# Block-sparse attention and a two-layer MoE in one kernel: four heads' denominators in one matmul group, row maxima moved by DMA, a shorter weight conversion and a new order of work

## The chip, the cores and the metric

One core of one Trainium2 chip runs the whole kernel. The metric is device time in microseconds (us); lower is better. Matrix multiplies run on TensorE (PE), whose weight loads the profile lists on their own (PEld); element-wise work runs on VectorE (DVE), ScalarE (ACT) and GpSimd (POOL); SyncE (SP) issues all DMAs from one queue, in order.

## The reference, cut to what matters

```python
B, H, S, D = 4, 8, 768, 64            # batch, heads, sequence, head dimension; blocks of 32
scores = q @ k.T / sqrt(D)
mask = band | first and last block row and column | 3 sampled blocks per block row
scores = where(mask, scores, -1e9); scores -= max(scores, axis=-1)
attn = exp(scores); attn /= sum(attn, axis=-1) + 1e-9
x = (attn @ v) put together to (B*S, 512)
h = x @ w_in                           # 512 -> 2048
out = (h * clip(h + 3, 0, 6) / 6) @ w_out   # 2048 -> 512
```

q, k and v come as 32-bit floats; w_in and w_out come as 64-bit floats and are turned into a high and a low 32-bit part on the chip.

## The kernel before, in words

The kernel makes products of 32-bit numbers from pairs of parts (hi and lo) in TensorE's fp32r form, and uses plain fp32 matmuls, which the trace shows as two records each, where the weights of the softmax are summed.

**Attention** is cut into 64 units u0 to u63: one head of one half of the queries of one batch, the head counting fastest. Eight units share a batch and a half. A unit loads q, k and v (loadq, loadk, loadv), splits them (qh, kh, qb on ACT, ql on DVE, kl on POOL into KB), and then:

- m_0 to m_2: scores of 128 queries each against all 768 keys, for the block maxima; the weights of these matmuls are QA, the moving side is KA (L611 to 620).
- r_0 to r_2, fin_0, fin_1: DVE reduces them to maxima of 24 blocks, adds the block mask and reduces to the negated maximum of each query, a 128x3 tile MN (mneg).
- mt and qm: three matmuls of MN against the identity turn the maxima into a row in PSUM, and ACT copies it into row 96 of QB (L638 to 644). There are two MN tiles and two QB tiles for each half.
- s_0 to s_2, e_0 to e_2: scores with the keys on the partitions, two matmuls per block of 128 keys: KA with QA, and KB with QB. The second brings in the low parts, the mask (rows 64 to 87) and the negated maximum (row 96). ACT takes the exponential.
- av: the product with v. In the first WIDE = 16 units the weights are 128 columns wide, v beside ones, so that the denominators come out of the same matmuls. From u16 on v alone, 64 columns, is laid on the two halves of the array in turn, and DVE sums the exponentials over the key blocks (suma, sumb, sumc).
- From u16 on, dm sums those over the partitions with a 128x64 matrix of ones, two heads (a pair) to the two column halves, dc copies to SBUF, and rc takes the reciprocal of 128x384 on DVE. Pairs in the list COMPACT gather one row per head to 128x6 by DMA first (rg), take the reciprocal of that, write it to DRAM (rs) and read it back spread over 64 partitions (rb).
- ux_0 to ux_2 multiply and split the result x for the MoE.

**The MoE** is cut into 64 steps m0 to m63: eight steps of two chunks of 128 hidden columns for each batch and half. h_ is x by w_in (hi by hi, lo by hi, hi by lo), ga, gb, gh and gl are the gate and its split on ACT, DVE, ACT and POOL, and o_ is the product with w_out into three output banks. The high parts of the weights stay in SBUF. The low parts are written to DRAM and loaded again for each step (loadin, loadout, four buffers each), except that chunks in the list DIRECT stay where they are for the first use.

**The weights** are 32 chunks w0 to w31 (L478 to 523): load the 64-bit words, size (ACT, absolute value of the high word), clamp (DVE), bits_0 to bits_2 (DVE, integer operations that put the bits of the 32-bit number together), high (ACT), low (the subtraction that leaves the low part; on POOL, or on DVE for chunks in the list QUICK), save (DMA).

**The order** is a text, SCORE, that names unit or step and operation one after the other; every engine and the DMA queue get their instructions in the order of this text, and nothing reorders them after. PSUM holds two big tiles of two banks for scores, MoE hidden columns, maxima and denominators, one bank for av and three for the output. An engine's instruction that waits holds up all behind it, and this holds for SyncE's DMAs as well.

All operations are recorded by one helper, so that the profile puts them all on line L359; they are told apart by the tiles that they write and read.

Of the kernel before, what the change touches and what calls it, by code (L numbers as in the profile page):

```python
# [908 lines left out]
```

## Time and profile before

| | us |
|---|---|
| three runs | 1034.07, 1035.63, 1036.9 (median 1035.63) |
| the profiled execution | 1036.67 |
| its span, first to last instruction | 1034.9 |
| PE busy in it | 985.5 (95%) |
| DVE, ACT, POOL busy | 711.8 (69%), 503.8 (49%), 279.8 (27%) |
| DMA moved | 148.27 MB, mean 143 GB/s |

A row of instruction groups reads: line, engine, operation, tiles written <- read, shape, count, then total busy us, mean ns of one, and the engine's idle time before them with what ended it. A row in order of time has the start in us, the duration and the same names. Matmuls overlap each other, so the spacing of their starts, not their duration, tells what one costs.

### The profile page before, as it was taken

What the parts mean: (1) busy time and instruction counts of PE and PEld (TensorE: products, weight loads), DVE (VectorE), ACT (ScalarE), POOL (GpSimd) and SP (SyncE); (2) the same over time, 40 slices, a digit from 0 to 9 for tenths busy, and PEclk for the clock granted to TensorE, in tenths of its full rate; (3) what the DMA queues carried; (4) which work ended last, traced back from release to release, by engine and by line L of the source; (5) the groups of instructions that cost most, each with busy time, mean ns of one, the idle gap of its engine ahead of it and who ended that gap; (6) DMA issues with size and microseconds to landing.
All of it is one profiled execution on the core that took longest, in us unless ns stands there. A gap on an engine that the chain in (4) does not pass through costs nothing.

```text
span 1034.9 us, 13289 instructions
## 1 busy us (share of the span) xinstructions
PE 985.5 (95%) x4904; PEld 783.4 (76%) x4904; DVE 711.8 (69%) x929; ACT 503.8 (49%) x781; POOL 279.8 (27%) x172
## 2 busy tenths in 40 slices
PE   4888999999999999999999999999999999999998
PEld 3565677778777777877888777778788877778986
DVE  5888789797667687677665768675867767864111
ACT  5677666555545454545443553453554455443121
POOL 4232334333223132222221322222222222221222
PEclk9998899999999999999999999999999999999999
DMA  5666657685534444433553444434434444413432
GB/s 159 189 185 198 186 188 211 208 259 159 168 100 120 145 142 133 135 102 120 142 166 99 136 128 145 127 111 120 153 112 132 133 136 152 123 58 106 143 112 91
DMA packets 119668, 148.27 MB, mean 143 GB/s; under 512 B 59667, under 2 KB 68755, under 8 KB 119604
## 3 DMA queue, kind: packets, MB, share of 16 engines
q1 hardware_dynamic: 119604, 147.44, 47.4%
q8 instruction: 38, 0.62, 0.3%
q14 instruction: 26, 0.21, 0.1%
HBM read 132.69 MB, written 14.70 MB: 142 GB/s over the span
## 4 chain that ended last, share of the span: by engine, by line
PE 70%; DVE 15%; DMA 5%; issue 4%; ACT 4%; SPq 0%; POOL 0%; POOLq 0%; DVEq 0%; ACTq 0%
PE big L359 41%; PE out L359 20%; PE av L359 10%; DVE xhl L359 5%; DVE acc L359 4%; DVE bm L359 2%; DVE rec L359 1%; ACT pr L359 1%; DMA kraw<-kT 1%; DMA wraw<-w_out 1%; DMA win_lo<-xhl 1%; DMA qraw<-qT 1%; DVE g L359 1%; DVE QA L359 1%; DMA wraw<-w_in 1%
## 5 line engine op out<-in xcount | busy, mean ns | idle before, releaser
L359 PE MATMUL big<-xhl,win_hi 128*128 128x384 f32 x1024 | 268.2, 343 | 1.9 <-DVE bm L359 1.9
L359 POOL TENSOR_TENSOR glo<-g,ghi 128x768 fp32r<-128x768 f32 x64 | 119.2, 1863 | 413.8 <-ACT ghi L359 401.3
L359 POOL TENSOR_TENSOR kb<-kraw,KA 64x768 fp32r<-64x768 f32 x64 | 124.8, 1950 | 273.2 <-ACT KA L359 238.2
L359 PEld LDWEIGHTS big<-xhl,win_hi 128*128 128x128 f32 x1024 | 183.0, 188 | 18.6 <-issue 7.8
L359 DVE TENSOR_REDUCE bm<-big 128x24 f32<-128x768 f32 x168 | 158.6, 953 | 55.8 <-PE big L359 53.7
L359 ACT ACTIVATE pr<-big 128x768 f32<-128x768 f32 x192 | 152.0, 811 | 87.8 <-PE big L359 86.5
L359 PE MATMUL av<-pr,vo 128*64 128x384 f32 (+1 forms) x768 | 176.7, 496 | 0.4 <-ACT pr L359 0.4
L359 PE MATMUL big<-xhl,wlo_in 128*128 128x384 f32 x512 | 172.3, 336 | 0.0
L359 PE MATMUL out<-wout_hi,ghi 128*128 128x512 f32 x384 | 154.1, 401 | 0.0
L359 PE MATMUL out<-wout_hi,glo 128*128 128x512 f32 x384 | 151.9, 396 | 0.2 <-POOL glo L359 0.2
L359 PE MATMUL out<-wlo_out,ghi 128*128 128x512 f32 x384 | 151.8, 395 | 0.0
L359 PE MATMUL big<-QA,KA 128*128 128x384 f32 x384 | 140.4, 366 | 4.6 <-ACT pr L359 3.8
L359 PE MATMUL big<-qb,kb 97*128 97x384 f32 x384 | 136.0, 354 | 4.6 <-ACT qb L359 4.6
L359 DVE SCALAR_TENSOR_TENSOR g<-g,big 128x768 f32<-128x768 f32 x64 | 60.8, 951 | 101.7 <-ACT g L359 101.4
L359 PEld LDWEIGHTS av<-pr,vo 128*64 128x64 f32 (+1 forms) x768 | 75.7, 152 | 64.4 <-issue 45.5
L359 PE MATMUL big<-KA,QA 128*128 128x384 f32 x336 | 92.9, 364 | 21.9 <-ACT xhl L359 11.4
L359 ACT ACTIVATE g<-big,half_b 128x768 f32<-128x768 f32 x64 | 57.7, 902 | 104.6 <-PE big L359 96.4
L359 PEld LDWEIGHTS big<-KA,QA 128*128 128x128 f32 x336 | 59.4, 192 | 53.5 <-issue 13.3
L359 PEld LDWEIGHTS big<-xhl,wlo_in 128*128 128x128 f32 x512 | 96.2, 188 | 0.0
L359 PEld LDWEIGHTS big<-QA,KA 128*128 128x128 f32 x384 | 75.8, 198 | 20.6 <-ACT pr L359 9.6
L359 DVE TENSOR_TENSOR acc<-pr 128x768 f32<-128x768 f32 x48 | 52.4, 1091 | 55.9 <-ACT pr L359 55.3
L359 PEld LDWEIGHTS out<-wout_hi,glo 128*128 128x128 f32 x384 | 72.1, 188 | 17.6 <-POOL glo L359 0.6
(67 smaller groups left out, 1136.1 us busy)
## 6 DMA issues: line engine op xcount, KB each, us to landing
wlo_out<-wout_lo SPq DMA_DIRECT2D x125, 256.0 KB, 2.7
wlo_in<-win_lo SPq DMA_DIRECT2D x120, 256.0 KB, 2.7
kraw<-kT SPq DMA_DIRECT2D x64, 384.0 KB, 3.5
qraw<-qT SPq DMA_DIRECT2D x64, 192.0 KB, 2.8
vo<-vP SPq DMA_DIRECT2D x64, 192.0 KB, 3.0
wraw<-w_out SPq DMA_DIRECT2D x16, 512.0 KB, 4.3
wraw<-w_in SPq DMA_DIRECT2D x16, 512.0 KB, 4.0
out_dram<-wraw SPq DMA_DIRECT2D x24, 256.0 KB, 2.9
```

The source lines that it names most:

```text
L359: return lambda *a, **k: tc.keep_in_program_order(op(*a, **k))
```

## The change

- The first 12 units, not 16, have the wide av.
- Denominators: the four heads of a quad (units 4i to 4i+3) are summed by four matmuls with 32 columns of ones, each onto the 32 partitions that belong to its head, after the sums of all four. Beyond the first 12 units the reciprocal always goes the compact way: four DMAs gather one row per head to 128x12, DVE takes the reciprocal of that, one DMA writes it to DRAM, and each pair reads its two rows back with two broadcasting DMAs. All six pairs of the wide units are in COMPACT. The buffers acc and uu grow to 5 and 4.
- Row maxima: a matmul m_t takes the queries t, t+3, t+6 and so on, so that partition p of MN holds queries 3p to 3p+2. From unit 10 on (BYDMA) one DMA writes the 128x3 maxima into row 96 of QB; the three matmuls and ACT's copy remain for units 0 to 9.
- Weights: size multiplies the high word by 2 to the power -112 instead of taking its absolute value; clamp is gone; bits_0 only shifts, and bits_2 takes the sign alone. All 32 subtractions (low) run on DVE, and only chunks 0 to 3 are used directly.
- SCORE is new from beginning to end.

```diff
-WIDE = 16
-QUICK = "4 6 8 14 17 18 22 30"
-DIRECT = "0 2 3 4 10 11 12 16 18 23 28"
-COMPACT = "1 3 5 7 13 21"
+WIDE = 12
+BYDMA = 10
+QUICK = "0 1 2 3 4 5 6 7 8 9 10 11 12 13 14 15 16 17 18 19 20 21 22 23 24 25 26 27 28 29 30 31"
+DIRECT = "0 1 2 3"
+COMPACT = "1 3 5 7 9 11"
 SCORE = """
...
-    ones = const.tile([P, D], F32, name="ones")
-    MN = [const.tile([P, NT, 2], F32R, name=f"mneg{i}") for i in range(2)]
+    ones = const.tile([P, 32], F32, name="ones")
+    MN = [const.tile([P, 2, NT], F32R, name=f"mneg{i}") for i in range(2)]
...
         def size(self):
...
-            act.activation(out=self.wf, in_=self.raw[:, :, 1].bitcast(F32), func=AF.Abs)
-
-        def clamp(self):
-            dve.tensor_scalar(out=self.wf, in0=self.wf, scalar1=2.0 ** -15, scalar2=None, op0=ALU.max)
+            act.mul(out=self.wf, in_=self.raw[:, :, 1].bitcast(F32), mul=2.0 ** -112)
...
-                dve.tensor_scalar(out=wi, in0=wi, scalar1=0x07FFFFFF, scalar2=3, op0=ALU.bitwise_and, op1=ALU.logical_shift_left)
+                dve.tensor_scalar(out=wi, in0=wi, scalar1=3, scalar2=None, op0=ALU.logical_shift_left)
...
             if op == "dm":
-                out.append((prev, "sumc"))
+                out += [(at(units, self.n - i), "sumc") for i in (3, 2, 1)]
+            if op == "rb" and not self.wide:
+                before = ""
+                out.append((self.last, "rs"))
+            if op == "mt" and self.n >= BYDMA:
+                before += " qb"
...
-                pe.matmul(out_j, lhsT=self.QA[:, t * P:(t + 1) * P], rhs=self.KA[:, j * HALF:(j + 1) * HALF], start=True, stop=True)
+                pe.matmul(out_j, lhsT=self.QA[:, t:HALF:NT], rhs=self.KA[:, j * HALF:(j + 1) * HALF], start=True, stop=True)
...
         def mt(self):
+            if self.n >= BYDMA:
+                dma.dma_start(out=self.QB[96:97].bitcast(F32).rearrange("o (p t) -> o p t", t=NT), in_=MN[self.n % 2].bitcast(F32)[:, 0])
+                return
             self.mtp = big_tile()
...
         def qm(self):
-            act.copy(out=self.QB[96:97], in_=self.mtp[0:1, 0, :HALF])
+            if self.n < BYDMA:
+                act.copy(out=self.QB[96:97].rearrange("o (p t) -> o t p", t=NT), in_=self.mtp[0:1, 0, :HALF].rearrange("o (t p) -> o t p", t=NT))
...
         def dm(self):
+
             self.den = big_tile()[:, 0, :HALF]
-            for side, acc in enumerate(pair_accs.pop(self.pair)):
-                pe.matmul(self.den[64 * side:64 * side + 64], lhsT=ones, rhs=acc, start=True, stop=True)
+            for i, acc in sorted(quad_accs.pop(self.quad).items()):
+                pe.matmul(self.den[32 * i:32 * i + 32], lhsT=ones, rhs=acc, start=True, stop=True)
...
         def rg(self):
 
-            if self.n in compact:
-                self.spread = sb.tile([P, HALF // 64], F32, name="spread")
-                for i in (0, 64):
-                    dma.dma_start(out=self.spread[i:i + 64], in_=self.rec[i:i + 1].rearrange("o (a c) -> o a c", a=64))
+            heads = 2 if self.wide else 4
+            if self.n in compact or not self.wide:
+                self.spread = sb.tile([P, heads * HALF // P], F32, name="spread")
+                for i in range(heads):
+                    p0 = P // heads * i
+                    dma.dma_start(out=self.spread[p0:p0 + P // heads], in_=self.rec[p0:p0 + 1].rearrange("o (a c) -> o a c", a=P // heads))
...
         def rb(self):
...
+            row, each, first = self.row if self.wide else self.last.row, 64 if self.wide else 32, 0 if self.wide else self.n % 4 - 1
+            if not self.wide:
+                self.rec = sb.tile([P, HALF], F32, name="rec")
+            for i in range(2):
+                one = row[each * (first + i):each * (first + i + 1)].rearrange("a c -> (a c)").rearrange("(o n) -> o n", o=1)
+                dma.dma_start(out=self.rec[64 * i:64 * i + 64], in_=one.to_broadcast([64, HALF]))
```

In the built program the order below is read engine by engine. Each row is one instruction, or several equal ones in a row; the names are the tiles' names, with a buffer number where two rows would read alike, and L359 of the kernel before is L356 after.

More of the change, by code (lines that the diff above doesn't have):

```diff
@@ L464, in mq @@
             for t in range(NC):
-                pe.matmul(self.mqp[:, 0, t * NB:(t + 1) * NB], lhsT=self.ind_r[:, t * P:(t + 1) * P], rhs=self.mval[:, 64:88], start=True, stop=True)
+                pe.matmul(self.mqp[:, 0, t * NB:(t + 1) * NB], lhsT=self.ind_r[:, t // NT * HALF + t % NT:(t // NT + 1) * HALF:NT], rhs=self.mval[:, 64:88], start=True, stop=True)
         def rows(self):
@@ L478, in fused_kernel @@
     class Weight(Work):
-        NEEDS = {"size": "load", "clamp": "size", "bits_0": "clamp", "bits_1": "bits_0", "bits_2": "bits_1", "high": "bits_2", "low": "high", "save": "low"}
+        NEEDS = {"size": "load", "bits_0": "size", "bits_1": "bits_0", "bits_2": "bits_1", "high": "bits_2", "low": "high", "save": "low"}
         def __init__(self, src, hi, lo_d):
@@ L507, in bits @@
             else:
-                dve.scalar_tensor_tensor(out=wi, in0=high, scalar=-0x40000000, in1=wi, op0=ALU.bitwise_and, op1=ALU.bitwise_or)
+                dve.scalar_tensor_tensor(out=wi, in0=high, scalar=-0x80000000, in1=wi, op0=ALU.bitwise_and, op1=ALU.bitwise_or)
         def high(self):
@@ L548, in __init__ @@
             self.early = 0 < n <= H
+            self.quad = (b, h // 4, hf)
         def needs(self, op):
@@ L666, in sumc @@
         def sumc(self):
-            self.acc = sb.tile([P, HALF], F32, name="acc", bufs=3)
-            pair_accs.setdefault(self.pair, []).append(self.acc)
+            self.acc = sb.tile([P, HALF], F32, name="acc", bufs=5)
+            quad_accs.setdefault(self.quad, {})[self.n % 4] = self.acc
             dve.tensor_tensor(out=self.acc, in0=self.acc2[:, 0], in1=self.acc2[:, 1], op=ALU.add)
@@ L686, in uc @@
             if self.side == 0:
-                pair_u[self.pair] = sb.tile([P, HALF], F32, name="uu")
+                pair_u[self.pair] = sb.tile([P, HALF], F32, name="uu", bufs=4)
             act.copy(out=pair_u[self.pair][self.mine], in_=self.avt[self.mine])
@@ L846, in fused_kernel @@
     units = [Unit(n, *u) for n, u in enumerate(units)]
+    for x in units:
+        x.last = units[x.n // 4 * 4 + 3]
     steps = [Step(n, n // NFP // 2, n // NFP % 2, n % NFP) for n in range(NU)]
```

589 lines of the change are left out of this document (292 added, 297 removed).

## The prediction

> **What bounds the kernel now.** I read the page's first lines, then the busy time by stage, then the groups of instructions, and last the order of time inside the long middle stage. The page says which engine is full:
>
> ```profile
> PE 985.5 (95%) x4904; PEld 783.4 (76%) x4904; DVE 711.8 (69%) x929; ACT 503.8 (49%) x781; POOL 279.8 (27%) x172
> ```
>
> TensorE matmuls (PE) are in flight 95% of the span, but that is an average. The busy time by stage (columns: stretch, its length, then PE, weight loads, VectorE, ScalarE, GpSimd with their counts, granted clock, DMA share, GB/s) splits it:
>
> ```profile
> 0.00:260.00 260.00, 224.31 (x958) 172.41 (x959) 208.87 (x321) 158.03 (x255) 90.09 (x72) 0.96 0.64 195
> 260.00:936.00 676.00, 666.15 (x3479) 527.94 (x3478) 482.64 (x585) 323.59 (x499) 169.44 (x89) 1.00 0.43 128
> 936.00:1035.00 99.00, 94.98 (x471) 83.01 (x469) 20.30 (x23) 22.21 (x28) 20.27 (x11) 1.00 0.36 112
> ```
>
> In the first 260 us, where the weights are converted, PE idles 35.7 us, VectorE (DVE) is busy 80% and the clock is 0.96; none is full, and steps wait for each other. From 260 to 936 us PE idles 9.9 us of 676: this stage is bound by the number and length of matmuls. From 936 on there is only MoE work, which the change leaves alone. So the rule for the sum is: a matmul removed after 260 us is worth its full spacing, DVE and ScalarE time removed there is worth little, and in the first stage a saving counts only in part.
>
> The profiled execution took 1036.67 us, 1.8 more than its span of 1034.9; the median of the three runs is 1035.63. I sum against 1036.67.
>
> **The change part by part.** First the path of the row maxima, one unit of it in order of time (start, duration, engine):
>
> ```profile
> 506.15 0.96 DVE L359 TENSOR_REDUCE bm<-big 128x24 f32<-128x768 f32 x1 [0.54 <-PE big L359]
> 506.18 0.39 PE L359 MATMUL out<-wlo_out,ghi 128*128 128x512 f32 x1
> 506.41 0.39 PE L359 MATMUL out<-wout_hi,glo 128*128 128x512 f32 x1
> 507.14 0.23 DVE L359 TENSOR_TENSOR bm<-bm,mq 128x72 f32<-128x72 f32 x1
> 507.41 0.23 DVE L359 TENSOR_REDUCE mneg<-bm 128x3 fp32r<-128x72 f32 x1
> 509.46 0.34 PE L359 MATMUL big<-ident,mneg 128*2 128x128 f32 x3
> 509.64 0.57 PE L359 MATMUL big<-xhl,win_hi 128*128 128x384 f32 x2
> 509.84 0.47 ACT L359 CAST qb<-big 1x384 fp32r<-1x384 f32 x1 [0.48 <-PE big L359]
> 510.75 0.34 PE L359 MATMUL big<-QA,KA 128*128 128x384 f32 x1
> 510.93 0.34 PE L359 MATMUL big<-qb,kb 97*128 97x384 f32 x1
> ```
>
> The maxima are ready 0.23 us after 507.41. Three small matmuls move them to a row (start 509.46), the next ordinary matmul starts at 509.64, so they take 0.18 us of PE, and ScalarE's copy ends at 510.31. The scores start afterwards; their matmuls are 0.18 us apart (510.75, 510.93), and the wider ones of the MoE output 0.23 (506.18, 506.41). The change does this for units 10 to 63 by a DMA. Removed: 54 x 0.18 = 9.7 us of PE. Where these matmuls and their copies go, PE, before (unit 24 and, behind it, unit 23; QB of unit 24 is qb_108):
>
> ```order
> L359 MATMUL big<-ident,mneg_117 2x128 x3
> L359 MATMUL big<-xhl,win_hi 128x384 x2
> L359 MATMUL big<-xhl,wlo_in 128x384
> L359 MATMUL big<-xhl,win_hi 128x384 x2
> L359 MATMUL big<-xhl,wlo_in 128x384
> L359 MATMUL big<-ident,mneg_118 2x128 x3
> L359 MATMUL big<-xhl,win_hi 128x384 x2
> L359 MATMUL big<-xhl,wlo_in 128x384
> L359 MATMUL big<-xhl,win_hi 128x384 x2
> L359 MATMUL big<-xhl,wlo_in 128x384
> L359 MATMUL big<-QA,KA 128x384
> L359 MATMUL big<-qb_108,kb_110 128x384
> ```
>
> And after, the end of the stretch that leads to unit 24's scores:
>
> ```order
> L356 MATMUL big<-qb_107,kb_111 128x384
> L356 MATMUL out_2394<-wout_hi,ghi 128x512
> L356 MATMUL out_2394<-wlo_out,ghi 128x512
> L356 MATMUL out_2394<-wout_hi,glo 128x512
> L356 MATMUL out_2395<-wout_hi,ghi 128x512
> L356 MATMUL out_2395<-wlo_out,ghi 128x512
> L356 MATMUL out_2395<-wout_hi,glo 128x512
> L356 MATMUL av<-pr,vo_120 64x384 x6
> L356 MATMUL big<-acc,ones 32x384 x4
> L356 MATMUL big<-QA,KA 128x384
> L356 MATMUL big<-qb_108,kb_110 128x384
> ```
>
> The identity matmuls have gone, and the denominators come as four heads of 32 columns. Between unit 24's last score block for the maxima and its first row of qb_108 now stand 12 score matmuls (12 x 0.18 = 2.2 us), 9 of the output (9 x 0.23 = 2.1), one set of AV and one denominator.
>
> ```profile
> L359 PE MATMUL big<-acc,ones 128*64 128x384 f32 x96 | 26.1, 501 | 1.3 <-DVE acc L359 1.1
> L359 PE MATMUL av<-pr,vo 128*64 128x384 f32 x576 | 104.7, 494 | 0.0
> L359 PE MATMUL av<-pr,vo 128*128 128x384 f32 x192 | 71.9, 504 | 0.4 <-ACT pr L359 0.4
> L359 PE MATMUL big<-ident,mneg 128*2 128x128 f32 x192 | 22.2, 225 | 8.4 <-DVE mneg L359 8.4
> L359 PEld LDWEIGHTS big<-acc,ones 128*64 128x64 f32 x96 | 7.2, 135 | 13.5 <-issue 6.0 <-DVE acc L359 5.9 <-ACT qb L359 0.4
> L359 DVE RECIPROCAL rec<-rec 128x384 f32<-128x384 f32 x26 | 66.3, 2550 | 14.4 <-ACT rec L359 14.1
> ```
>
> PE stood 8.4 us before the identity matmuls until the maxima were ready; of this, between 260 and 936 us (waits: total, times, longest):
>
> ```profile
> PE big L359 <- DVE mneg L359: 1.4, 3, 0.7
> ```
>
> I count only these 1.4 us.
>
> Denominators: 96 records for 24 pairs take 26.1 us, 1.09 a pair in flight. In order of time one pair takes less:
>
> ```profile
> 834.05 0.81 PE L359 MATMUL big<-acc,ones 128*64 128x384 f32 x4
> 834.80 0.44 PE L359 MATMUL big<-QA,KA 128*128 128x384 f32 x1
> 835.55 2.55 DVE L359 RECIPROCAL rec<-rec 128x384 f32<-128x384 f32 x1 [0.22 <-ACT rec L359]
> ```
>
> Four records start at 834.05 and the next matmul at 834.80: 0.75 us for two heads, though one record alone lasts 0.50; so the two column tiles ran beside each other. If four tiles of 32 columns do the same, a group of four heads costs what a pair did. 24 pairs at 0.75 to 1.09 become 13 groups (units 12 to 63) at the same: 11 x 0.75 to 11 x 1.09, 8.3 to 12.0 us; I take 10, nearer the group's mean since some pairs are torn apart by a wait. Weight loads of ones waited 5.9 us for the sums (DVE acc); with 13 places instead of 24, and the quad's first three sums long done, I take 3 of it as saved.
>
> The Trainium skill, page "TensorEngine Tiling (Array Packing)", section "Key Properties", says that a change of tiling mode drains the array. A 32-column group behind a 64-column AV would pay this where today's pair runs on. No row shows that switch; at the 0.18 us that a whole group of narrow identity matmuls takes, 13 of them would give 2.3 us back.
>
> AV: units 12 to 15 leave the 128-column form. 71.9 us / 16 = 4.49 a unit, against 104.7 / 48 = 2.18: 4 x 2.31 = 9.2 us. They lie in the first stage, where PE has idle time, so the worth is between 0 and 9.2; I take 4.
>
> The reciprocals of 128x384 (66.3 us of DVE) shrink to small ones, as do ScalarE's copies of the maxima and half the denominator copies. After 260 us PE hides all of it: worth 0. What is late in its place is the trip through DRAM:
>
> ```profile
> spread<-rec SPq DMA_DIRECT2D x12, 1.5 KB, 3.2
> rec<-spread SPq DMA_DIRECT2D x6, 3.0 KB, 2.6
> ```
>
> Two hops of some 3 us and a broadcast, which the pairs in COMPACT make already. The first MoE step that reads the result comes several units later; worth 0.
>
> Weight conversion, first stage, in rows of DVE and GpSimd:
>
> ```profile
> L359 DVE TENSOR_SCALAR xhl<-xhl 128x512 f32<-128x512 f32 x32 | 17.0, 531 | 7.8 <-ACT xhl L359 7.4
> L359 POOL TENSOR_TENSOR xhl<-xhl,wout_hi 128x512 f32<-128x512 f32 x12 | 15.3, 1288 | 24.5 <-issue 12.2 <-ACT wout_hi L359 11.7 <-POOL kb L359 0.6
> L359 DVE TENSOR_TENSOR xhl<-xhl,win_hi 128x512 f32<-128x512 f32 x5 | 6.0, 1201 | 0.0
> L359 DVE TENSOR_TENSOR wlo_in<-xhl,win_hi 128x512 fp32r<-128x512 f32 x2 | 1.4, 692 | 0.6 <-ACT win_hi L359 0.5
> L359 DVE TENSOR_TENSOR acc<-acc,pr 128x768 f32<-128x768 f32 x48 | 59.4, 1238 | 15.1 <-ACT pr L359 13.2
> L359 DVE TENSOR_TENSOR acc<-pr 128x768 f32<-128x768 f32 x48 | 52.4, 1091 | 55.9 <-ACT pr L359 55.3
> L359 DVE TENSOR_TENSOR acc<-acc 128x384 f32<-128x384 f32 x48 | 45.1, 940 | 1.4
> L359 DVE TENSOR_TENSOR uu<-av,tmp 64x384 f32<-64x384 f32 x48 | 26.5, 553 | 8.1 <-ACT tmp L359 6.9
> ```
>
> Removed on DVE: 32 clamps, 17.0 us, and three reciprocals of 2.55 (pairs ending with units 9, 11, 15), 7.7. Added: 24 subtracts that GpSimd did (1.29 each), at 0.69 to 1.20: 16.6 to 28.8; and the sums and merges of units 12 to 15, 4 x (1.09 + 1.24 + 0.94 + 0.55) = 15.3. Net +7 to +19 us on DVE over 260, against 24 x 1.29 = 31 us less on GpSimd. The first chunk before, on DVE:
>
> ```order
> L359 TENSOR_TENSOR bm<-bm,mq 128x72
> L359 TENSOR_REDUCE mneg_117<-bm 128x3
> L359 TENSOR_SCALAR xhl<-xhl 128x512 x3
> L359 SCALAR_TENSOR_TENSOR xhl<-wraw,xhl 128x512 x2
> L359 TENSOR_SCALAR xhl<-xhl 128x512
> L359 SCALAR_TENSOR_TENSOR xhl<-wraw,xhl 128x512 x2
> ```
>
> And after:
>
> ```order
> L356 TENSOR_TENSOR bm<-bm,mq 128x72
> L356 TENSOR_REDUCE mneg_117<-bm 128x3
> L356 SCALAR_TENSOR_TENSOR xhl<-wraw,xhl 128x512
> L356 TENSOR_SCALAR xhl<-xhl 128x512
> L356 SCALAR_TENSOR_TENSOR xhl<-wraw,xhl 128x512
> L356 TENSOR_TENSOR wlo_in<-xhl,win_hi 128x512
> L356 SCALAR_TENSOR_TENSOR QA<-qraw,QA 64x384
> ```
>
> The clamp has left the chain of TENSOR_SCALARs and the subtract into wlo_in has joined behind the last bit operation: the chain of one weight chunk no longer goes round by GpSimd. A chunk's chain gets shorter (0.53 and 0.6 less), DVE's queue a little longer. I take 0 for the first stage, between -15 (if half of PE's 35.7 us of idle time goes with the shorter chain) and +12 (if two thirds of the added DVE time shows).
>
> The new cost is the DMA for the maxima. It stands in SyncE's one queue, here for unit 24:
>
> ```order
> L356 DMA wlo_in<-win_lo_89 128x512
> L356 DMA vo_119<-vP 128x6x64
> L356 DMA wlo_out<-wout_lo_102 128x512
> L356 DMA qb_108<-mneg_117 1x128x3
> L356 DMA qraw<-qT 128x384
> L356 DMA vo_120<-vP 128x6x64
> L356 DMA spread<-rec 32x1x12 x4
> L356 DMA kraw<-kT 128x768
> ```
>
> The transfer of qb_108 stands behind a load of low weights, which waits until PE has read the old ones, and ahead of the next q, v and k loads, which it holds up until the maxima are ready; those are wanted a unit later. How long the queue stands at such loads today:
>
> ```profile
> SPq L359 <- PE big L359: 239.9, 131, 7.5
> SPq L359 <- PE out L359: 236.7, 108, 10.6
> ```
>
> That is 239.9/131 = 1.8 and 236.7/108 = 2.2 us each. The need from the last block of scores to the landed row: 0.96 + 0.23 + 0.23 and a landing like the small spread's, 3.2: 4.6 us. Cover for unit 24: 2.2 + 2.1 + 2.2 (AV) + 0.75 = 7.2 us. Counting rows in the same way, most units have 6 to 10 us and the least two (19 and 63) some 4.9. So it is mostly hidden, and shows at the narrow ones if a load of 2 us holds the queue. I take 3 us in all, from 0 to 54 x 0.5 = 27.
>
> Last, the weight side of the maxima's own matmuls now steps over three columns (QA at stride 3). No row here shows a strided weight load. Below nothing is excluded (no work is removed). Bound by the rows that exist:
>
> ```profile
> L359 PEld LDWEIGHTS big<-KA,QA 128*128 128x128 f32 x336 | 59.4, 192 | 53.5 <-issue 13.3 <-ACT xhl L359 11.4 <-DVE bm L359 10.0
> L359 PEld LDWEIGHTS av<-pr,vo 128*64 128x64 f32 x576 | 38.6, 136 | 47.7 <-issue 43.7 <-ACT QA L359 1.0 <-DVE acc L359 0.7
> L359 PEld LDWEIGHTS big<-ident,mneg 128*2 128x2 f32 x192 | 13.1, 83 | 22.9 <-DVE mneg L359 8.6 <-issue 6.9 <-PE av L359 1.2
> ```
>
> 83 ns for 2 columns, 136 for 64, 192 for 128: about 0.85 ns a column, so reading at half speed would add 0.11 us to each of 6 x 64 = 384 loads, 42 us if all of it shows, 14 if a third of it does, 0 if the load still ends under the matmul before. I take 0. The Trainium skill, page "SBUF — State Buffer", in the note on cachelines in the section "Door 1: The DMA port swizzle", speaks against the change: lines are 16 bytes and at least two hits on a line are wanted, and 12-byte steps give four accesses in three lines; the same note calls strides up to 4 fp32 free. By the first half the sum would rise by the strided rival's price below, by the second by nothing.
>
> Sum: 1036.7 - 9.7 - 1.4 - 10 - 3 - 4 + 0 + 3 = 1011.6, so 1011.
>
> **The rivals.** (a) The first stage gains as well: shorter chunk chain, GpSimd off the shared work, -15: 996. For it: PE idle there 35.7 us; against: DVE gets 7 to 19 us more to do. (b) The first stage loses: +12, 1023. (c) The strided loads show by a third: +14, 1025; wholly, +42, 1053. (d) The four 32-column tiles do not run beside each other, so that the change does not do what it says: two tiles at a time cost 13 more pairs, 13 x 0.75 = 10 us, one at a time about 20: 1021 to 1031. (e) The other side: the maxima land late. Each unit whose landing exceeds its cover stops PE at the first row of qb; 54 units at 0.52 us eat all 28.1 us, at 1 us they make 1036.7 - 28.1 + 54 = 1063. With a cover of 7.2 it decides at a landing of 7.2 - 1.4 + 0.5 = 6.3 us after the maxima instead of 3.2, that is if the queue usually stands 3 us more with them ready. Against it: the loads ahead mostly wait for PE work that stands before the scores anyway.
>
> **How the numbers follow.** Forecast 1011, chance 0.58; (a) 0.13; (b) 0.08; (c) 0.07 by a third and 0.02 wholly; (d) 0.03; (e) 0.09. A difference under 0.3% (3.1 us) is about what a measurement of this kernel cannot tell from none. Faster by more: the forecast, (a), (b), the milder (c) and (d): 0.89. Within: (e) where it just eats the gain, 0.05. Slower: the rest of (e) and (c) wholly, 0.06. The range reaches from (a), 996, past (b) and the milder (c) into (d), 1028; the unknown costs (AV 0 to 9, denominators 8 to 12, maxima 0 to 27) lie in it but for the end of the last.
>
> **What would show it.** Right: no identity matmuls after unit 9; denominators in 13 groups with eight records in about 0.75 us; PE idle after 260 us still about 10 us and that stage about 20 us shorter; 384-column matmuls for the maxima still 0.18 apart; landing of the mneg row about 3 us. Wrong: PE waits for the DMA of qb that sum to over 10 us, weight loads of QA above 0.2 us with matmuls spread to match, or a first stage whose 260 us move by more than 12.

## The result, and the profile after

Four runs of the changed kernel took 998.31 to 1003.93 us, median 999.4, beside 1034.07 to 1036.9, median 1035.47, of the kernel before: ratio 0.966, 95% interval 0.9627 to 0.9692. That is 11.6 us below the forecast of 1011, near rival (a), a first stage that gains as well. The profiled execution took 998.31 us, span 996.5, against 1036.67 and 1034.9. The engines, from the page:

```profile
PE 954.3 (96%) x4750; PEld 772.0 (77%) x4750; DVE 649.4 (65%) x924; ACT 468.2 (47%) x712; POOL 248.8 (25%) x148
```

To compare stages they have to end at the same work. I cut both traces at the first matmul of MoE step m9 and of step m57. The first cut is not quite the same work: ahead of it the changed kernel has the 12 score matmuls of unit 17, some 2.2 us at 0.18 each, which the kernel before has behind it. The busy time by stage, before:

```profile
0.00:256.80 256.80, 221.11 (x939) 169.31 (x940) 207.16 (x319) 157.56 (x254) 88.69 (x72) 0.96 0.64 195
256.80:954.60 697.80, 687.95 (x3595) 546.67 (x3594) 492.03 (x596) 330.64 (x509) 174.53 (x92) 1.00 0.43 127
954.60:1035.00 80.40, 76.39 (x373) 67.39 (x372) 12.64 (x15) 15.64 (x18) 16.58 (x9) 1.00 0.38 118
```

And after:

```profile
0.00:244.20 244.20, 214.33 (x935) 166.09 (x936) 194.06 (x326) 153.53 (x245) 58.03 (x48) 0.96 0.71 216
244.20:917.00 672.80, 664.15 (x3446) 538.61 (x3446) 442.70 (x584) 299.04 (x449) 174.17 (x91) 1.00 0.48 138
917.00:997.00 80.00, 75.80 (x373) 67.28 (x371) 12.65 (x15) 15.64 (x18) 16.57 (x9) 1.00 0.40 119
```

The first stage is 12.6 us shorter, the middle 25.0, and the rest, up to the spans' ends, 0.8 (80.3 against 79.5). With unit 17's scores on the same side of the cut it would be some 15 and 23. In the middle PE's idle time is 9.9 us before and 8.7 after: the gain there is hardly idle time, but matmuls that are gone or start closer together. In the first stage PE idles 35.7 us before and 29.9 after, and VectorE (DVE), which my sum loaded with 7 to 19 us more, is busy 13.1 us less.

The groups of instructions that the sum spoke of, after (busy, mean ns, then idle time ahead of them):

```profile
L356 PE MATMUL big<-acc,ones 128*32 128x384 f32 x104 | 13.6, 498 | 0.9 <-DVE bm L356 0.8
L356 PE MATMUL av<-pr,vo 128*64 128x384 f32 x624 | 112.1, 494 | 0.0
L356 PE MATMUL big<-ident,mneg 128*2 128x128 f32 x30 | 5.0, 279 | 3.0 <-DVE mneg L356 2.9
L356 PE MATMUL big<-qb,kb 97*128 97x384 f32 x384 | 135.0, 352 | 8.9 <-ACT qb L356 7.7 <-DMA qb<-mneg 1.0
L356 PEld LDWEIGHTS big<-acc,ones 128*32 128x32 f32 x104 | 2.6, 108 | 8.7 <-issue 3.5 <-DVE acc L356 2.3 <-DVE bm L356 1.1
L356 DVE RECIPROCAL spread<-spread 128x12 f32<-128x12 f32 x13 | 2.9, 224 | 2.4 <-DMA spread<-rec 2.3
```

13 groups of eight records stand where 24 pairs of four stood, 30 identity matmuls are left of 192, and for the rows that come by DMA PE waits 1.0 us in all. In order of time, a denominator group of four heads behind AV:

```profile
437.20 0.34 PE L356 MATMUL big<-xhl,wlo_in 128*128 128x384 f32 x1
437.46 2.16 PE L356 MATMUL av<-pr,vo 128*64 128x384 f32 x12
439.55 0.85 PE L356 MATMUL big<-acc,ones 128*32 128x384 f32 x8
440.33 0.62 PE L356 MATMUL big<-xhl,win_hi 128*128 128x384 f32 x2
```

Four heads take 0.78 us (439.55 to 440.33), where two took 0.75. Inside the group the four tiles start 7 ns apart, so they do run beside each other. What waits in SyncE's queue (total, times, longest), and the landing (KB, median us):

```profile
SPq L356 <- PE big L356: 173.5, 111, 7.7
SPq L356 <- PE out L356: 154.7, 100, 9.4
SPq L356 <- DVE mneg L356: 36.4, 27, 3.0
```

```profile
qb<-mneg SPq DMA_DIRECT2D x54, 1.5 KB, 2.4
```

The queue stands 36.4 us for the maxima, but less for PE than before (239.9 and 236.7 us), and the rows land after 2.4 us, sooner than the 3.2 that I took.

### The profile page after: what moved, and what is told of

Same layout as the page of the kernel before. It is cut to its first block, busy times and chain, and to the rows that moved or that the text cites. A ratio compares the mean times of both kernels' runs of the same rounds, so it can differ in the third digit from the quotient of the medians.

```text
span 996.5 us, 13217 instructions
## 1 busy us (share of the span) xinstructions
PE 954.3 (96%) x4750; PEld 772.0 (77%) x4750; DVE 649.4 (65%) x924; ACT 468.2 (47%) x712; POOL 248.8 (25%) x148
## 4 chain that ended last, share of the span: by engine, by line
PE 83%; DVE 6%; ACT 4%; issue 3%; DMA 3%; POOL 0%; SPq 0%; DVEq 0%; ACTq 0%; POOLq 0%
PE big L356 46%; PE out L356 24%; PE av L356 13%; DVE acc L356 2%; DVE bm L356 2%; DMA wraw<-w_out 1%; ACT pr L356 1%; ACT qb L356 1%; DMA wout_lo<-xhl 1%; DVE xhl L356 1%; DVE QA L356 1%; ACT rec L356 0%; DMA qb<-mneg 0%; ACT g L356 0%; DMA spread<-rec 0%
## 5 line engine op out<-in xcount | busy, mean ns | idle before, releaser
L356 PE MATMUL big<-xhl,win_hi 128*128 128x384 f32 x1024 | 264.0, 339 | 2.7 <-DVE bm L356 2.1
L356 POOL TENSOR_TENSOR glo<-g,ghi 128x768 fp32r<-128x768 f32 x64 | 118.7, 1855 | 477.2 <-ACT ghi L356 456.8
L356 DVE TENSOR_REDUCE bm<-big 128x24 f32<-128x768 f32 x168 | 158.6, 954 | 82.0 <-PE big L356 80.8
L356 ACT ACTIVATE pr<-big 128x768 f32<-128x768 f32 x192 | 152.0, 812 | 123.6 <-PE big L356 123.0
L356 PEld LDWEIGHTS big<-xhl,win_hi 128*128 128x128 f32 x1024 | 185.5, 188 | 14.5 <-DVE bm L356 6.0
L356 POOL TENSOR_TENSOR kb<-kraw,KA 64x768 fp32r<-64x768 f32 x64 | 124.7, 1948 | 254.5 <-ACT KA L356 208.2
L356 PE MATMUL big<-xhl,wlo_in 128*128 128x384 f32 x512 | 173.1, 338 | 0.0
L356 PE MATMUL av<-pr,vo 128*64 128x384 f32 (+1 forms) x768 | 166.1, 498 | 0.0
L356 PE MATMUL out<-wout_hi,ghi 128*128 128x512 f32 x384 | 152.8, 398 | 0.0
L356 PE MATMUL out<-wout_hi,glo 128*128 128x512 f32 x384 | 151.7, 395 | 0.0
L356 PE MATMUL out<-wlo_out,ghi 128*128 128x512 f32 x384 | 150.7, 392 | 0.0
L356 PE MATMUL big<-QA,KA 128*128 128x384 f32 x384 | 139.3, 363 | 5.9 <-ACT pr L356 2.8
L356 PE MATMUL big<-qb,kb 97*128 97x384 f32 x384 | 135.0, 352 | 8.9 <-ACT qb L356 7.7
L356 ACT ACTIVATE g<-big,half_b 128x768 f32<-128x768 f32 x64 | 57.7, 902 | 159.7 <-PE big L356 145.9
L356 DVE SCALAR_TENSOR_TENSOR g<-g,big 128x768 f32<-128x768 f32 x64 | 60.8, 949 | 95.1 <-ACT g L356 94.8
L356 PEld LDWEIGHTS av<-pr,vo 128*64 128x64 f32 (+1 forms) x768 | 69.2, 149 | 65.6 <-issue 50.9
L356 PE MATMUL big<-KA,QA 128*128 128x384 f32 x336 | 93.8, 370 | 12.5 <-DVE QA L356 10.4
L356 DVE TENSOR_TENSOR acc<-pr 128x768 f32<-128x768 f32 x52 | 57.9, 1113 | 69.3 <-ACT pr L356 69.2
L356 PEld LDWEIGHTS big<-KA,QA 128*128 128x128 f32 x336 | 75.6, 255 | 33.6 <-issue 13.3
L356 PEld LDWEIGHTS big<-xhl,wlo_in 128*128 128x128 f32 x512 | 96.1, 188 | 0.3 <-DMA wlo_in<-win_lo 0.3
L356 PEld LDWEIGHTS big<-QA,KA 128*128 128x128 f32 x384 | 74.9, 195 | 27.2 <-ACT pr L356 8.4
L356 ACT CAST ghi<-g 128x768 fp32r<-128x768 f32 x64 | 53.3, 833 | 79.4 <-DVE g L356 54.0
```

Source lines behind the costliest of these rows:

```text
L356: return lambda *a, **k: tc.keep_in_program_order(op(*a, **k))
```

## The experiments

Each run's ratio to the kernel before on the same chip is the measure: its distance to the changed kernel is its ratio less 0.966, times 1035.6 us. That 0.966 is itself uncertain by 3.4 us, so differences below some 4 us need the trace as well. The old order has to be told from the new one throughout, since both can carry the parts.

**The maxima over PE again (e1_identity).** In the new order, identity matmuls and ScalarE's copy for all 64 units; in SCORE the mt and qm of units 10 to 63 move nearer to their scores.

```diff
-BYDMA = 10
+BYDMA = ()
...
-            if self.n >= BYDMA:
+            if self.n in BYDMA:
...
-            if self.n < BYDMA:
+            if self.n not in BYDMA:
```

> The changed kernel with the row maxima moved by the three identity matmuls and ScalarE's copy in every unit, as before, at places in the new order that lie 2 to 8 us of PE work behind the unit's last maxima block; all else as after. Theory (the matmuls were worth their spacing on a full TensorE): 54 x 0.18 = 9.7 us come back, less the 1.5 us for which PE waits for the landed row of qb in the changed kernel: 1006 to 1010 us. Rival 1 (they ran in gaps that PE has anyway, and the new order alone gave the gain): 998 to 1002 us. Rival 2 (the old way also brings back waits for the maxima, 8.4 us in the whole run before): 1012 to 1018 us.

1029.24 us, ratio 0.9933 (0.9911 to 0.9954): 28.3 us above the changed kernel, above every theory's range. In the profiled execution, the longest of the ten with 1034.55 us, PE waited 20.1 us, 28 times, for qb. Part of these waits may be my placing's; the next kernel moves it.

**The same, better placed (e5_identity_moved).** Apart from the way in which BYDMA is written (64 here, with the tests as in the changed kernel), only the places of mt and qm in SCORE differ from e1_identity.

> As e1_identity (maxima by identity matmuls in every unit of the changed kernel), but each unit's three matmuls stand where, by the spacings of the trace, 2.9 us of PE work lie between the last maxima block and them, at least 1.5 us between them and the scores, and 1.1 us before another score, MoE or denominator block needs a PSUM tile; ScalarE's copy follows them at once. In e1_identity PE waited 20.1 us for qb (8.1 in the changed kernel) and 8.3 us for the maxima (2.9). Theory A (work of 9.7 us, the waits were my placing): 1008 to 1013 us. Theory B (the row's way over PE takes a third claim on the two big PSUM tiles, and costs waits wherever it stands): 1018 to 1029 us.

1026.82 us, ratio 0.9915 (0.989 to 0.994): 26.4 us above the changed kernel; theory B. By stage:

```profile
0.00:246.30 246.30, 215.33 (x958) 166.04 (x959) 192.56 (x326) 158.51 (x253) 57.63 (x48) 0.97 0.71 214
246.30:944.40 698.10, 680.03 (x3585) 544.32 (x3584) 435.64 (x584) 330.65 (x495) 172.58 (x91) 1.00 0.46 133
```

and the wait for the row and its neighbours:

```profile
PE big L362 <- ACT qb L362: 12.1, 16, 1.5
PE big L362 <- DVE QA L362: 8.9, 3, 7.4
```

The middle is as long as before the change, 698.1 us, and 25.3 longer than the changed kernel's. From matmul start to matmul start, the 46 units there spend 16.4 us from the first identity matmul to what follows, against 8.5 for as many units in the kernel before; the other 8.9 us are spread over the matmuls around. In the old order, 46 of the 48 groups of units 16 to 63 give way after 0.18 us, nearly all to MoE matmuls; in this one 14 of 48 last over 0.3 us, 12 of them with a maxima or score block of another unit behind them, which needs one of the two big PSUM tiles. Six last 1.08 us: the matmul behind reads neither maxima nor row, but starts only when ScalarE's copy of the row (ACT qb) has freed the tile:

```profile
482.76 0.34 PE L362 MATMUL big<-ident,mneg 128*2 128x128 f32 x3
483.14 0.65 ACT L362 CAST qb<-big 1x384 fp32r<-1x384 f32 x1 [0.43 <-PE big L362]
483.85 0.44 PE L362 MATMUL big<-QA,KA 128*128 128x384 f32 x1 [0.74 <-ACT qb L362]
```

The other eight, 0.37 to 0.80 us, end with VectorE's or ScalarE's reading of the other tile (bm, g or pr). Placing with more care won 2 us, which is less than the two runs can tell apart; at these places the rest stays. Whether an order made for these matmuls could avoid it, as the old one does, no run shows.

**The work without the tile (e9_extra_matmuls).** Three narrow matmuls a unit, into unused columns of AV's bank, for nobody:

```diff
-                self.avt = avp.tile([P, HALF], F32, name="av")
+                both = avp.tile([P, DM], F32, name="av")
+                self.avt = both[:, :HALF]
+                if self.n >= BYDMA:
+                    for t in range(NT):
+                        pe.matmul(both[0:2, HALF:], lhsT=ident[:, 0:2], rhs=ident, start=True, stop=True)
```

> The changed kernel with three matmuls more ahead of the AV of each unit from 10 on: two columns of the identity as weights, the identity as the moving side, into 128 unused columns of AV's own bank, read by nobody. They cost what the identity matmuls of the maxima cost TensorE, without their claim on one of the two big PSUM tiles, without ScalarE's copy and without a wait for the maxima. Bringing those back whole cost 27 to 30 us. Theory (the work alone is worth its spacing, the rest was the tile and the waits): 54 x 0.18 = 9.7 us more than the changed kernel, 1007 to 1011 us. Rival 1 (narrow matmuls fall into gaps): 998 to 1002 us. Rival 2 (the narrow groups disturb the stream and are dear by themselves): 1014 us and more.

1003.6 us, ratio 0.9703 (0.9681 to 0.9725): 4.5 us more, between the theory and rival 1. The trace tells which, cut at the same steps:

```profile
0.00:241.70 241.70, 213.27 (x956) 165.27 (x957) 194.58 (x326) 152.93 (x245) 57.83 (x48) 0.97 0.72 218
241.70:922.10 680.40, 672.21 (x3587) 549.26 (x3587) 443.30 (x584) 299.01 (x449) 173.91 (x91) 1.00 0.47 137
922.10:1002.00 79.90, 75.79 (x373) 67.27 (x371) 12.64 (x15) 15.62 (x18) 16.57 (x9) 1.00 0.38 119
```

The middle is 7.6 us longer (680.4 against 672.8) for 141 matmuls more, 47 units at 0.16: there the work is worth nearly its spacing. The first stage of this execution is 2.5 us shorter than that of the changed kernel's profiled one, although it has more to do. In the profiled executions of the changed kernel, of this one, e11_straight_weights and e12_subtract_gpsimd that stage ends at 244.2, 241.7, 243.2 and 241.4 us, so some 3 us of it vary without a cause that shows.

**The DMA in the old order (e7_dma_old_order).** The kernel before with this part alone; in SCORE each mt of units 10 to 63 moves right behind fin_1, or behind qb where that is later, and qm goes:

```diff
+BYDMA = 10
...
-                pe.matmul(out_j, lhsT=self.QA[:, t * P:(t + 1) * P], rhs=self.KA[:, j * HALF:(j + 1) * HALF], start=True, stop=True)
+                pe.matmul(out_j, lhsT=self.QA[:, t:HALF:NT], rhs=self.KA[:, j * HALF:(j + 1) * HALF], start=True, stop=True)
...
         def mt(self):
+            if self.n >= BYDMA:
+                dma.dma_start(out=self.QB[96:97].bitcast(F32).rearrange("o (p t) -> o p t", t=NT), in_=MN[self.n % 2].bitcast(F32)[:, 0])
+                return
```

> The kernel before with the row maxima by DMA from unit 10 on (strided queries, no identity matmuls), each transfer put in SyncE's queue right behind the maxima, all else and the order as before. In the old order the PE work between the last maxima block and the scores is 2.4 to 17.5 us (median 6.5) by the spacings, against 4.9 to 13.7 (median 7.8) in the new one. Theory (9.7 us of matmuls go, some 4 to 6 us come back at the eight units whose cover is under 0.96 + 0.23 + 0.23 + 2.4 = 3.8 us): 1028 to 1033 us. Rival (the waits for the landed row, and loads held up in SyncE's queue, eat all of it): 1035 to 1050 us. Rival (removed matmuls free the PSUM tiles as well and are worth more): under 1025 us.

1045.09 us, ratio 1.0104 (1.0068 to 1.014): 10.8 us slower than the kernel before; the first rival. PE's waits:

```profile
PE big L359 <- DMA qb<-mneg: 14.2, 14, 2.4
PE big L359 <- DVE mneg L359: 5.5, 7, 1.5
```

14.2 us of waits for the row eat the 9.7 us of matmuls. This profile shows the fastest of the four executions, 1040.05 us; the others took up to 1047.98, and no trace shows where. This is the prediction's rival (e): the part is a loss in the old order, whose work between maxima and scores goes down to 2.4 us, and a gain in the new one, where it is 4.9 at the least. But the cover is not all of it. Counted by the spacings, ten of the 14 waits, 9.5 us, are at units with less cover than 4.9 us; the other four, 4.7 us, are at units with 4.9 to some 9 (15, 22, 28 and 50). In the changed kernel the one long wait, 1.0 us, is at unit 16, which has over 8.

**Denominators by pairs (e2_pairs).**

```diff
-    ones = const.tile([P, 32], F32, name="ones")
+    ones = const.tile([P, D], F32, name="ones")
...
-            for i, acc in sorted(quad_accs.pop(self.quad).items()):
-                pe.matmul(self.den[32 * i:32 * i + 32], lhsT=ones, rhs=acc, start=True, stop=True)
+            for side, acc in enumerate(quad_accs.pop(self.pair)):
+                pe.matmul(self.den[64 * side:64 * side + 64], lhsT=ones, rhs=acc, start=True, stop=True)
```

In SCORE, the odd units 13, 17 and so on get dm, dc and rc behind their own sums; rg, rs and rb do nothing from unit 12 on.

> The changed kernel with the denominators taken by pairs of heads again from unit 12 on (two matmuls with 64 columns of ones in 26 places, and a reciprocal of 128x384 on VectorE, no trip through DRAM); all else as after. Theory (four 32-column tiles run beside each other, so half of the groups went): 13 groups more at 0.75 to 1.09 us are 10 to 14 us, so 1009 to 1014 us. Rival 1 (the change from 64-column AV tiles to 32-column tiles drains the array, so that a quad costs nearly two pairs): under 4 us more, 999 to 1003 us. Rival 2 (VectorE's 26 reciprocals of 2.55 us, 66 us more, delay the sums and maxima, so that PE waits for them as well): over 1018 us.

1041.62 us, ratio 1.0039 (1.002 to 1.0058): 39.2 us above the changed kernel; rival 2, and by far more than PE's work. The reciprocals and the waits:

```profile
L363 DVE RECIPROCAL rec<-rec 128x384 f32<-128x384 f32 x26 | 66.3, 2548 | 4.9 <-ACT rec L363 4.7
```

```profile
PE big L363 <- DVE QA L363: 17.6, 9, 7.1
PE big L363 <- DVE bm L363: 13.5, 15, 2.5
PE big L363 <- ACT qb L363: 7.4, 10, 1.5
PE big L363 <- ACT rec L363: 5.9, 8, 1.0
```

**Pairs with the small reciprocal (e6_pairs_compact).** As e2_pairs, with every pair gathered, inverted and read back by its own rg, rc, rs and rb; acc has four buffers instead of five.

```diff
-COMPACT = "1 3 5 7 9 11"
+COMPACT = "1 3 5 7 9 11 13 15 17 19 21 23 25 27 29 31 33 35 37 39 41 43 45 47 49 51 53 55 57 59 61 63"
```

> As e2_pairs (denominators by pairs, 26 groups of two heads), but every pair's reciprocal goes the compact way over 128x6 and DRAM, so that VectorE's 26 reciprocals of 2.55 us are gone. In e2_pairs PE waited 17.6 us for QA, 13.5 for bm and 3.9 for g, all VectorE's (10.4, 4.6 and 0.7 in the changed kernel), and 5.9 us for rec (0.9), which is ScalarE's copy of the sums. Theory A (13 groups more cost PE work of 10 to 14 us and 5 us for the copy, the rest was the reciprocals): 1013 to 1020 us. Theory B (groups of 64 columns cost three times what I counted, reciprocals or not): 1030 to 1042 us. Rival C (the groups cost nothing, all was the reciprocals): 998 to 1004 us.

1015.54 us, ratio 0.982 (0.9785 to 0.9856): 16.6 us above the changed kernel; theory A. The groups and the wait for the copy:

```profile
L365 PE MATMUL big<-acc,ones 128*64 128x384 f32 x104 | 24.8, 504 | 2.9 <-DVE bm L365 2.0 <-DVE g L365 0.7 <-DVE acc L365 0.2
```

```profile
PE big L365 <- ACT rec L365: 5.9, 8, 1.0
```

So e2_pairs' 39 us were some 17 for 13 groups more, 1.3 us each, and some 23 for reciprocals of 2.55 us that stand ahead of maxima and query splits on VectorE. A step that I had called free "since PE hides all of it" is free only at places that suit it.

**The weight conversion (e4_new_conversion_old_order, e3_old_conversion, e12_subtract_gpsimd).** The first is the kernel before with the new conversion, the second the changed kernel with the old one; their edits are these lines, with the shift and masks of the bit operations, in one direction or the other:

```diff
-            act.activation(out=self.wf, in_=self.raw[:, :, 1].bitcast(F32), func=AF.Abs)
-        def clamp(self):
-            dve.tensor_scalar(out=self.wf, in0=self.wf, scalar1=2.0 ** -15, scalar2=None, op0=ALU.max)
+            act.mul(out=self.wf, in_=self.raw[:, :, 1].bitcast(F32), mul=2.0 ** -112)
...
-QUICK = "4 6 8 14 17 18 22 30"
+QUICK = "0 1 2 3 4 5 6 7 8 9 10 11 12 13 14 15 16 17 18 19 20 21 22 23 24 25 26 27 28 29 30 31"
```

> The kernel before with the new weight conversion alone (no clamp, all 32 subtractions on VectorE), in the old order. Theory (conversion shortens the first stage by itself): 6 to 12 us less than before, 1024 to 1030 us. Rival 1 (only the new order can use it): 1033 to 1038 us. Rival 2 (VectorE, with 17 to 29 us of subtractions more, delays the maxima and sums that stand behind them in the old order): 1038 to 1048 us.

1031.94 us, ratio 0.9953 (0.9936 to 0.997): 4.9 us less than the kernel before, somewhat less than the theory's 6 to 12 and clear of no change; m9 starts 4.9 us earlier (251.9 against 256.8), and the middle is as long as before.

> The changed kernel with the old weight conversion (absolute value, clamp on VectorE, masks in the bit operations) and with 24 of the 32 subtractions on GpSimd again, in the new order. Theory (the shorter chain of a chunk shortened the first stage, whose end moved from 257 to 244 us): that stage gets 6 to 12 us longer, 1005 to 1011 us, and the rest stays. Rival (the new order and the 4 units less with wide AV shortened the first stage, the conversion did nothing, as my sum had it): 998 to 1002 us.

1004.67 us, ratio 0.9688 (0.9662 to 0.9713): 2.9 us above the changed kernel, just short of the theory; that ratio alone cannot tell it from none.

> The changed kernel with 24 of the 32 subtractions of the weights on GpSimd again, and the new conversion otherwise (no clamp). Old conversion and old place of the subtractions together cost 5.3 us in the new order. Theory A (GpSimd's subtractions slow VectorE's steps beside them, from 0.47 to 0.59 and from 0.70 to 0.84 us a bit operation, and lengthen a chunk's chain): 1002 to 1006 us. Theory B (the clamp was what cost): 999 to 1001 us. Rival (VectorE relieved of 17 to 29 us is worth more): under 998 us, and then it is the better kernel.

```diff
-QUICK = "0 1 2 3 4 5 6 7 8 9 10 11 12 13 14 15 16 17 18 19 20 21 22 23 24 25 26 27 28 29 30 31"
+QUICK = "4 6 8 14 17 18 22 30"
```

998.35 us, ratio 0.966 (0.9628 to 0.9693): no difference, nearest to theory B. Its first stage, and behind it that of e3_old_conversion, which has the old absolute value, clamp and masks besides:

```profile
0.00:241.50 241.50, 211.52 (x935) 164.36 (x936) 189.94 (x302) 153.46 (x245) 90.47 (x72) 0.97 0.71 219
```

```profile
0.00:246.90 246.90, 213.66 (x934) 164.00 (x935) 208.83 (x334) 154.00 (x245) 92.58 (x72) 0.97 0.70 214
```

In these two executions the old conversion with its clamp makes VectorE 18.9 us busier and the stage 5.4 us longer, of which some 3 can be the variation above; by the runs' ratios it is 2.9 us, within their intervals. Where the subtractions run makes no difference that these runs can tell.

**Sixteen units with wide AV (e10_wide16).**

```diff
-WIDE = 12
+WIDE = 16
-COMPACT = "1 3 5 7 9 11"
+COMPACT = "1 3 5 7 9 11 13 15"
```

In SCORE, units 12 to 15 get av_0, av_1, av_2, uc and dw for av, tt, uu and the sums, u15 loses dm and dc, u13 gets rg, rc and rs, and the loads of v for u14 to u17 come later.

> The changed kernel with 16 units with wide AV again: units 12 to 15 make their denominators in 128-column AV matmuls, their sums on VectorE (15 us) and the first group of four heads are gone, and units 13 and 15 gather by pairs; all else as after. Theory (4 x 2.31 = 9.2 us of AV less one group of 0.75 to 1.09, about half of it behind PE's idle time, as my sum had it): 3 to 6 us more, 1002 to 1006 us. Rival 1 (it counts in full): 1007 to 1010 us. Rival 2 (the first stage waits for VectorE anyway): 996 to 1001 us.

1005.8 us, ratio 0.9717 (0.9701 to 0.9733): 5.9 us more, at the upper end of the theory. Its profiled execution, 7.3 us longer than that of the changed kernel, has only half of this in the first stage (3.7 us, then 3.5):

```profile
0.00:247.90 247.90, 219.09 (x926) 171.85 (x927) 182.52 (x311) 154.94 (x248) 57.83 (x48) 0.96 0.69 213
247.90:924.20 676.30, 665.86 (x3446) 539.80 (x3445) 441.50 (x584) 299.09 (x449) 174.60 (x91) 1.00 0.47 138
```

Without these four units' sums VectorE is 11.5 us less busy in the first stage than in the changed kernel, and the stage is longer even so.

**Straight weights (e11_straight_weights).**

```diff
-                pe.matmul(out_j, lhsT=self.QA[:, t:HALF:NT], rhs=self.KA[:, j * HALF:(j + 1) * HALF], start=True, stop=True)
+                pe.matmul(out_j, lhsT=self.QA[:, t * P:(t + 1) * P], rhs=self.KA[:, j * HALF:(j + 1) * HALF], start=True, stop=True)
```

> The changed kernel with the maxima's weights read as 128 neighbouring columns of QA instead of every third column, so that the maxima go to other queries of the unit. The loads take 250 ns strided (median) and 187 straight. Theory (the load ends under the 0.18 us matmul before or is ahead of it, as the spacings of 0.177 and 0.179 us say): 998 to 1002 us. Rival 1 (a third shows): 384 x 0.063 / 3 = 8 us less, 990 to 993 us. Rival 2 (all of it shows): 24 us less, 974 to 977 us.

998.36 us, ratio 0.9646 (0.9626 to 0.9666): 1.4 us less, which is no difference; the theory. The loads, in the changed kernel and in this one:

```profile
L356 PEld LDWEIGHTS big<-KA,QA 128*128 128x128 f32 x336 | 75.6, 255 | 33.6 <-issue 13.3 <-DVE bm L356 7.1 <-ACT g L356 2.0
```

```profile
L361 PEld LDWEIGHTS big<-KA,QA 128*128 128x128 f32 x336 | 59.9, 190 | 37.2 <-issue 13.6 <-DVE bm L361 6.9 <-ACT g L361 2.1
```

**The head of the order (e8_head).** The kernel before with the first loads in the new order:

```diff
-    k0 ident; u0 loadq loadk; k0 table ind samp; u1 loadv; u0 loadv; w1 load; k0 index; w3 load; k0 allow;
+    k0 samp; u0 loadq loadk; k0 table; u1 loadv; u0 loadv; w1 load; k0 index; w3 load; k0 ind ident allow;
...
```

> The kernel before with one edit to the order: the load of the sampled blocks stands first, and the loads of the key rows and of the identity behind the first two weight chunks, as in the changed kernel. The first matmul starts at 11.4 us before and at 7.6 in the changed kernel; before, the sampled blocks land late, and VectorE's mask steps of 24x24 run beside GpSimd's casts, one of them for 2.64 us (0.22 in the changed kernel). Theory (the start is a delay of everything): 3 to 4 us less, 1031 to 1033 us. Rival (the first stage has slack for it): 1035 to 1037 us.

1034.94 us, ratio 0.9994 (0.9976 to 1.0012): nothing gained; the rival. The first matmul starts at 7.20 us instead of 11.42, but then PE waits for the mask rows, whose source now loads behind the weights:

```profile
PE big L365 <- DVE QA L365: 7.2, 1, 7.2
PE big L365 <- POOL ghi L365: 4.4, 1, 4.4
```

So this run moved a wait and did not remove it. In the changed kernel the same wait is 1.3 us, once; what its earlier start is worth there stays open.

## Why the prediction was right or wrong, point by point

**Where the time is bounded.** Right: after m9, a matmul more or less counts by its spacing (e9_extra_matmuls: 0.16 us a unit). The last stage moved by 0.8 us.

**Identity matmuls, 9.7.** Right in size. From start to start they took 13.9 us before and 4.9 after, 9.0 less. What my sum did not say is that this holds only for the two orders as they are: the DMA in the old order loses 10.8 us, the matmuls in the new order 26.4.

**Waits for the maxima, 1.4, and the DMA's price, 3.** Right. PE waits 1.0 us for the row of qb, its weight loads 0.5. The rival (e) was real: e7_dma_old_order is that mechanism. In the new order it does not show. Going by where e7_dma_old_order waits, the longer cover explains the greater part of that; 4.7 of its 14.2 us are at units whose cover is no shorter than the new order's least, and what keeps those away is open.

**Denominators, 10, and the waits of their weight loads, 3.** Right, if a little large: the sum had 13 for both. Over the run they take 10.8 us less from start to start (23.5 against 12.7), in the middle stage 11.9 (23.5 against 11.6), and what their weight loads wait for the sums falls from 5.9 to 2.3. e6_pairs_compact puts 16.6 us on 13 groups, 5 of them in PE's waits for ScalarE's copy of the sums (5.9 against 0.9), which holds one of the two big PSUM tiles. Rival (d) fell. As to the drain on a change of tiling: the last record of AV gives way after 0.32 us to a pair of 64 columns and after 0.42 to a group of 32 or a full matmul, so a change costs 0.10 us, and 13 of them 1.3 at most. The Trainium skill, page "TensorEngine Tiling (Array Packing)", section "Key Properties", says that a change of tiling mode drains the array; the trace agrees in so far as a change has that price.

**AV of units 12 to 15, 4 of 0 to 9.2.** Right in direction, too small: AV spends 10.6 us less from start to start in the first stage, and e10_wide16 puts 5.9 us on it, 3.7 of them in the first stage of its profiled execution.

**The first stage, 0 between -15 and +12.** This is the step that failed: the stage moved by 12.6 (some 15 with unit 17's scores on the same side), just past the 12 that the prediction had named as the sign of that. The sum had little more than 4 of it, under AV. The prediction let a shorter chain per chunk and a fuller VectorE cancel. Measured, the new conversion is worth 4.9 us by itself (e4_new_conversion_old_order), and VectorE got emptier by 13.1 us, not fuller by 7 to 19. The added subtractions cost 0.69 us each, the lower end of what I allowed; what the sum put at nothing are the bit operations, which together became 12.7 us shorter. The rows before and after:

```profile
L359 DVE SCALAR_TENSOR_TENSOR xhl<-wraw,xhl 128x512 int32<-128x512 int32 x64 | 53.4, 835 | 1.9
L359 DVE TENSOR_SCALAR xhl<-xhl 128x512 int32<-128x512 int32 x32 | 18.8, 587 | 0.9
```

```profile
L356 DVE SCALAR_TENSOR_TENSOR xhl<-wraw,xhl 128x512 int32<-128x512 int32 x64 | 44.4, 697 | 1.3
L356 DVE TENSOR_SCALAR xhl<-xhl 128x512 int32<-128x512 int32 x32 | 15.1, 473 | 7.9 <-ACT xhl L356 7.6
L356 DVE TENSOR_TENSOR xhl<-xhl,wout_hi 128x512 f32<-128x512 f32 x14 | 9.6, 686 | 0.7 <-ACT wout_hi L356 0.5
```

GpSimd's lighter load is about half of the cause: with 24 subtractions back on it, and all else as after, the same steps take

```profile
L361 DVE SCALAR_TENSOR_TENSOR xhl<-wraw,xhl 128x512 int32<-128x512 int32 x64 | 49.1, 772 | 1.4
```

But it would be wrong to give this the credit for the time: with the subtractions back on GpSimd the time is the same. Of the edits in the conversion, the clamp's going (with the new form of size and masks) is what is left to pay: 4.9 us in the old order, clear of no change, and 2.9 in the new one, which is not. Whether by a shorter chain or by 17 us less for VectorE to do, these runs do not separate. With AV's 3.7 to 5.9 and the conversion's 3 to 5, some 7 to 11 us of the first stage's 12.6 are accounted for. The rest is open: up to 3 us may be the variation of that stage, and the earlier start (e8_head), the shorter list DIRECT and the new order have a share that no run shows. So rival (a), 996, was near in time by luck in part: of its two reasons the shorter chain is worth 3 to 5 of its 15 us at most, and GpSimd off the shared work nothing that shows.

**Strided weights, 0.** Right. Each load takes 0.065 us longer, but the matmuls of the maxima still start 0.18 us apart, and none of it shows, so rival (c) fell. The Trainium skill, page "SBUF — State Buffer", section "Door 1: The DMA port swizzle", wants two hits on a cacheline of 16 bytes and also calls strides up to 4 fp32 free. For the duration of a load at a stride of 3 the first half holds here (255 against 190 ns), for the time of the kernel the second.

**Reciprocals and copies, 0.** Not shown by the change itself, but e2_pairs shows the size of what lay there: 26 reciprocals of 2.55 us cost some 23 us at places that an order has not been fitted to.

**What stays open.** The middle stage gained 25.0 us where the prediction said about 20. From start to start, the identity matmuls take 8.5 us less there and the denominators 11.9, much as the sum had it; beyond it the MoE's matmuls take 8.9 less (31 of their spacings, instead of 87, are more than 0.03 us over the usual 0.18 or 0.23), AV and the scores 4.3 more. That is the new order as a whole, which I did not try with the old parts, and no run changes DIRECT or the numbers of buffers alone. Taking parts back one at a time from the changed kernel costs 26.4 + 16.6 + 5.9 + 2.9 = 52 us, more than the 36 that the change brought, since a part that is put back into an order made without it brings its own waits.

## What to carry to other kernels

A part that trades engine work for latency, like the maxima by DMA, has no worth of its own: count the work between its start and its use in the order that it goes into, and it turns from +10.8 us to part of a gain. Removing one part and adding one part measure different things, so do both before a number is given to it. And where no engine is full, a conversion with an operation less in its chain is not worth zero: without 32 steps of 0.53 us, 17 us of VectorE, the old order was 4.9 us faster.

## What the runs showed of the hardware that was not expected

- A change of tile shape on TensorE costs 0.10 us of spacing (0.27 us from a full matmul to a 64-column one, 0.17 to 0.18 between full ones), whether or not narrow identity matmuls stand between: then the step is at their end (0.15 instead of 0.06).
- A small VectorE step can be stretched much beside GpSimd's work (seen, not tested by itself). At the start of the kernel before, beside GpSimd's casts, a step of 24x24 took 2.64 us; in the changed kernel and in e8_head, with the casts later, 0.22. Before:

```profile
7.08 0.87 POOL L359 CAST ghi<-pr 24x768 fp32r<-24x768 f32 x1
7.18 2.64 DVE L359 TENSOR_SCALAR eq<-tab,idxf 24x24 f32<-24x24 f32 x1
8.00 1.79 POOL L359 TENSOR_TENSOR kb<-kraw,KA 64x768 fp32r<-64x768 f32 x1
```

- A 128x3 tile that goes to one row of SBUF by DMA lands after 2.4 us (median of 54), sooner than the 256 KB loads in the same queue (2.8 and 2.9).
